# First batch of a spectral-filter and gated-FFN kernel: interleaved filter rows in larger pieces, the last two units loaded to both halves, one product on GpSimd

## Chip, cores and metric

One core of one Trainium2 chip. The time is device microseconds of one execution; "the loop" below is the long steady part that follows the first batch. The kernel before takes 782.3 us.

## The reference

```python
def _attn_ref(x, filt_r, filt_i):            # x (8, 3008, 256), filters (1505, 256), float32
    X = np.fft.rfft(x, axis=1)
    Y = X * (filt_r + 1j * filt_i)[None]
    return np.fft.irfft(Y, n=x.shape[1], axis=1).astype(np.float32)

def _moe_ref(x, w_in, w_out, beta):          # 24064 tokens, 256 -> 2048 -> 256
    h = x @ w_in
    g = h * (1.0 / (1.0 + np.exp(-beta * h)))
    return (g @ w_out).astype(np.float32)
```

The transforms are matmuls against sine tables made on the chip. Batch 0 goes through its transform first (the head, about 34 us). Then comes a loop of 752 steps, in which the FFN of one block runs beside the transform of the next batch.

## The kernel before

`fr_sb` and `fi_sb` hold the filters as [128 partitions, 24 rows, 256] float32. Partitions 0 to 63 and 64 to 127 carry the real and the imaginary part of the spectrum, so each filter value is needed in both halves. SyncE loads `fr` into the upper half and `fi` into the lower one; GpSimd copies each to the other half (`spread`). Six units of four rows go through VectorE. Further names: `t2` is one of the sine tables, `w_in` and `w_out` are the FFN's weights, `xg` is a piece of the second batch's input, Silu is the FFN's activation (one per loop step). An eviction is a copy of a matmul's result out of the accumulator memory, and the seam is the place where the head ends and the loop begins.

```python
    def load_filters(k0, k1):
        n = k1 - k0
        for filt, dst, p0 in ((filt_r, fr_sb, M), (filt_i, fi_sb, 0)):          # M = 64, H = 32
            for q0, off, sg in ((p0, k0, 1), (p0 + H, N1 - k0, -1)):
                src = AP(filt.tensor, filt.offset + off * D, [[N1 * D, H], [sg * D, n], [1, D]])
                nc.sync.dma_start(dst[q0 : q0 + H, k0:k1, :], src)
    ...
    for u in range(NUN):                                   # NUN = 6, KU = 4: 24 loads of 128 KB
        load_filters(u * KU, (u + 1) * KU)
    ...
    def s2_0(u):                                           # a unit: 4 matmuls, 2 products
        ...
        nc.vector.tensor_tensor(pq[u, 0][:], ps[:], fr_sb[:, ks, :], ALU.mult)
        nc.vector.scalar_tensor_tensor(pq[u, 1][:], ps[:], rot[:], fi_sb[:, ks, :], ALU.mult, ALU.mult)

    def spread(u):
        ks = slice(u * KU, (u + 1) * KU)
        nc.gpsimd.tensor_copy(fr_sb[:M, ks, :], fr_sb[M:, ks, :])
        nc.gpsimd.tensor_copy(fi_sb[M:, ks, :], fi_sb[:M, ks, :])

    for u in range(4):                                     # GpSimd's queue, in this order
        spread(u)
    load_win(0, 4 * P)                                     # w_in, cast to bf16 by the DMA
    spread(4)
    load_win(4 * P, FF)
    spread(5)
    for g in range(4):
        load_x(1, g)                                       # the second batch's input
    ...
    s2_0(3); unit(2); s2_0(4); a0_turn(5); ...; unit(3); s2_0(5); ...; unit(4)
```

Of the kernel before, what the change touches and what calls it, by code (L numbers as in the profile page):

```python
# [10 lines left out]
P = 128  # L11
# [10 lines left out]
N1 = 47  # L22
M = 64
# [13 lines left out]
def kernel(  # L37
# [45 lines left out]
    WZ = KP * J  # L83
    CH = M * J

    def load_filters(k0, k1):
        n = k1 - k0
        for filt, dst, p0 in ((filt_r, fr_sb, M), (filt_i, fi_sb, 0)):
            for q0, off, sg in ((p0, k0, 1), (p0 + H, N1 - k0, -1)):
                src = AP(filt.tensor, filt.offset + off * D, [[N1 * D, H], [sg * D, n], [1, D]])  # L90
                nc.sync.dma_start(dst[q0 : q0 + H, k0:k1, :], src)  # L91

    t1 = consts.tile([NP, KP], BF16, name="t1", tag="t1")
    t4 = consts.tile([KP, NP], BF16, name="t4", tag="t4")
# [46 lines left out]
    def iota(tile_, pattern, base=0, ch=0):  # L141
        nc.gpsimd.iota(tile_, pattern=pattern, base=base, channel_multiplier=ch)
# [39 lines left out]
    iota(kc[:], [[1, NK], [0, 2]])  # L182
    iota(cc[:], [[0, NK], [1, 2]], base=1)
    load_x0(8, 16)
    iota(vi[:, :, :H], [[1, NK], [N1, H]])
    load_x0(16, 24)
    iota(vi[:, :, H:], [[1, NK], [-N1, H]], base=N1 * (M - 1))
    load_x0(24, 28)
    make_identity(nc, ident)
    load_x0(28, 32)  # L190
# [2 lines left out]
    def shift_and(name, sh, mask, eng=None):  # L193
        t = small(name, I32)
        eng = eng or nc.vector
        if sh:
            eng.tensor_scalar(t[:], ip[:], sh, mask, ALU.logical_shift_right, ALU.bitwise_and)
        else:
            eng.tensor_scalar(t[:], ip[:], mask, None, ALU.bitwise_and)
        return t  # L200

    def affine(name, src, mul, add, eng=None):
        t = small(name)
        (eng or nc.vector).tensor_scalar(t[:], src[:], mul, add, ALU.mult, ALU.add)
        return t
# [10 lines left out]
    ms = affine("ms", shift_and("m_i", 0, M - 1), TURN / S, 0.0)  # L216
    off = affine("off", c_i, -TURN / 4, TURN / 4)
    q_i = shift_and("q_i", 0, 1)
    v_i = shift_and("v_i", 5, 1)
    q_p = (affine("q0", q_i, -1.0, 1.0), affine("q1", q_i, 1.0, 0.0))  # L220

    def t2_half(hi):
        t = sq.tile([P, NK, H], I32, name="u", tag=f"u{hi}")
        nc.vector.tensor_scalar(  # L224
            t[:], vi[:, :, hi * H : (hi + 1) * H], ms[:], off[:], ALU.mult, ALU.add
        )
        fold(t[:])
        nc.scalar.activation(
            t2[:, :, hi * H : (hi + 1) * H], t[:], ACT.Sin, scale=TWO_PI / TURN
        )  # L230

    def t2_shift(hi):
        for c in range(2):
            d0, s0 = (0, M) if c == 0 else (M, 0)
            dst = t2[d0 : d0 + M, :, M + hi * H : M + (hi + 1) * H]
            src = t2[s0 : s0 + M, :, hi * H : (hi + 1) * H]
            if c == hi:
                nc.vector.tensor_scalar_mul(dst, src, -1.0)
            else:
                nc.vector.tensor_copy(dst, src)  # L240

    MG = 4
    aTv = aT[:].rearrange("p e k (g m) -> p g e k m", m=MG)
# [64 lines left out]
    t2_half(1)  # L308
    seen = sp.tile([1, 2], BF16, name="seen", tag="seen")
    nc.sync.dma_start(seen[:], t2[:1, 1, M - 2 : M])  # L310
    for u in range(NUN):
        load_filters(u * KU, (u + 1) * KU)
    gp = nc.gpsimd
    rot = affine("rot", v_i, 2.0, -1.0, gp)
    tiny = sp.tile([P, NFB], F32, name="tiny", tag="tiny")
    gp.tensor_tensor(tiny[:], beta_sb[:], beta_sb[:], ALU.mult)
    gp.tensor_scalar(tiny[:], tiny[:], 1e-12, 2e-6, ALU.is_lt, ALU.mult)
# [1 line left out]
    s1_0(0, (False,))  # L319
    s1_0(1, (True,))  # L320
    spin(5, idle)
    t2_shift(0)
    t2_shift(1)
    nc.vector.memset(t2[:, 0, M : P : M - 1], 0.0)
    nc.scalar.activation(warm[:], ms[:], ACT.Silu)
    s1_0(2, (False,))
# [96 lines left out]
    r_p0 = ExitStack()  # L423
    p0pool = rpool("p0pool", r_p0, bufs=2, **tw)

    def s2_0(u):
        ps = bank2([P, KU, D])
        for i in range(KU):
            k1 = u * KU + i
            nc.tensor.matmul(ps[:, i, :], lhsT=t2[:, k1, :], rhs=a0[:, k1, :], start=True, stop=True)  # L430
        ks = slice(u * KU, (u + 1) * KU)
        for c in range(2):
            pq[u, c] = p0pool.tile([P, KU, D], BF16, name="pq_t", tag=f"pq{c}")
        nc.vector.tensor_tensor(pq[u, 0][:], ps[:], fr_sb[:, ks, :], ALU.mult)
        nc.vector.scalar_tensor_tensor(
            pq[u, 1][:], ps[:], rot[:], fi_sb[:, ks, :], ALU.mult, ALU.mult
        )
# [32 lines left out]
# [4 lines that stand above are left out]
# [6 lines left out]
    for u in range(4):  # L480
        spread(u)
    load_win(0, 4 * P)
    spread(4)
    load_win(4 * P, FF)
    spread(5)
    for g in range(4):
        load_x(1, g)
    load_wout(0)
    load_wout(WG)
    scale_wout(0)  # L490
    scale_wout(WG)

    s2_0(0)
    a0_turn(2)
# [3 lines left out]
    unit(0)  # L498
    a0_turn(3)
    s2_0(2)  # L500
    unit(1)
    a0_turn(4)
    s2_0(3)
    unit(2)
    s2_0(4)
    a0_turn(5)
    t3_part(2, True)
    t3_neg(2, True)
    unit(3)
    s2_0(5)  # L510
    idle = tpsum.tile([P, 512], F32, name="tps", tag="tps")
    spin(3, idle)
    unit(4)
    banks.close()

# [156 lines left out]
    for b in range(1, B):  # L672
        o = first_step[b - 1]
        if b == 1:
            at(0, z_late, 1, 0)
            at(1, z_late, 1, 1)
            s1_steps(1, range(16), [1 + (2 * i + 1) // 3 for i in range(16)], False, (1, 4, 7, 10, 13))
            for i, r in enumerate((11, 12, 13, 14)):
                at(r, f_late, 1, i // 2, i % 2)
            for g in range(NG):  # L680
                at(o + 13, a2_load, 1, g)
            for hh, z0, f0 in ((2, (13, 14), (15, 16, 17, 18)), (3, (18, 19), (20, 21, 22, 23))):
                for e in range(NDC):
                    at(z0[e], z_late, hh, e)
# [144 lines left out]
```

## Time and profile before

| kernel before | value | read from |
|---|---|---|
| time | 782.3 us (782.1 to 783.2) | runs |
| span of the profiled run | 780.2 us | page |
| filter loads land | 12.5 to 26.7 us | landing times in the trace |
| VectorE's last product of the head ends | 30.61 us | timeline |
| first transpose, first loop matmul | 31.44, 33.84 us | timeline of PE |
| granted clock | 1.00 throughout the head | stretches |

A timeline row gives the start, the duration, engine, line and operation, and in square brackets the idle time before it with what ended that. A "stretch" row gives the window, its length, busy time of PE, PE's weight loads, VectorE, ScalarE and GpSimd, then the granted TensorE clock, the DMA engines' busy share and GB/s. A DMA packet is called unslowed when it takes as long as between 42 and 45 us of this kernel: 159 ns (median) for 4096 bytes. The lines that carry the argument are in the prediction below.

### The profile page before, as it was taken

Reading aid. Unit: us, or ns where it says so; the run is one execution under the profiler, and the core shown is the slowest. Engines: PE = TensorE matmul, PEld = TensorE weight load, DVE = VectorE, ACT = ScalarE, POOL = GpSimd, SP = SyncE. Lnnn points to the kernel's source line nnn. Section 1 sums busy time; section 2 is a strip of 40 time slices with the busy share of each in tenths; the row PEclk is TensorE's granted clock in tenths of the full one; section 3 lists DMA queues with packets and bytes.
Section 4 is the critical chain, followed back from the end, with each engine's and each line's share of the span. In section 5 each row is a group of like instructions: output and inputs, shape, how many; then the busy total and the mean of one; then the engine's idle time right before and its main releaser. Section 6 shows DMA issues by size and latency. Waiting matters only on the chain.

```text
span 780.2 us, 15154 instructions
## 1 busy us (share of the span) xinstructions
PE 764.1 (98%) x5956; PEld 544.0 (70%) x6051; DVE 446.0 (57%) x713; ACT 552.6 (71%) x814; POOL 151.4 (19%) x155
## 2 busy tenths in 40 slices
PE   8899999999999999999999999999999999999997
PEld 5677667766776667866678666776667776676665
DVE  7869754766556665566546665567655666321001
ACT  6767877676677766777667776677766777777776
POOL 6714400312012210122201322022200222000000
PEclk9999999999999999999999999999999999999999
DMA  9975585244913358042671417622164111500101
GB/s 185 233 213 116 147 209 155 70 108 115 252 42 80 103 116 242 29 113 71 152 207 45 119 48 181 176 75 69 48 189 135 48 48 49 156 28 28 55 28 55
DMA packets 84411, 88.51 MB, mean 113 GB/s; under 512 B 5788, under 2 KB 74652, under 8 KB 84340
## 3 DMA queue, kind: packets, MB, share of 16 engines
q1 hardware_dynamic: 79892, 73.81, 32.0%
q0 software_dynamic: 4304, 13.60, 10.5%
q8 instruction: 47, 0.77, 0.4%
q14 instruction: 24, 0.20, 0.1%
q10 hardware_dynamic: 144, 0.13, 0.0%
HBM read 54.47 MB, written 46.66 MB: 130 GB/s over the span
## 4 chain that ended last, share of the span: by engine, by line
PE 94%; DMA 2%; issue 1%; POOL 1%; DVE 1%; SPq 0%; ACT 0%; DVEq 0%; POOLq 0%
PE acc L788 43%; PE hps L770 39%; PE ps L561 3%; PE ps L629 3%; PE ps L607 3%; PE ps L577 2%; DMA xg<-in_x_dram 1%; DMA fi_sb<-in_filt_i_dram 1%; POOL fi_sb L473 0%; POOL fr_sb L472 0%; SPq L91 0%; PE ps L405 0%; PE tp L400 0%; DVE y L114 0%; DVE u L224 0%
## 5 line engine op out<-in xcount | busy, mean ns | idle before, releaser
L779 ACT ACTIVATE gT<-hps,beta_sb 128x512 bf16<-128x512 f32 x752 | 516.9, 687 | 213.3 <-PE hps L770 191.9
L788 PE MATMUL acc<-wout_sb,gT 128*128 128x256 bf16 x3008 | 452.9, 272 | 2.3
L770 PE MATMUL hps<-y,win_sb 128*128 128x512 bf16 (+7 forms) x1636 | 428.0, 350 | 0.1
L788 PEld LDWEIGHTS <-gT 128*128 128x128 bf16 x3008 | 286.9, 98 | 121.6 <-issue 0.9
L596 POOL TENSOR_TENSOR yh<-a_t,b_t 128x512 bf16<-128x512 f32 x84 | 106.4, 1267 | 424.1 <-DVE b_t L595 422.8
L770 PEld LDWEIGHTS <-win_sb 128*128 128x128 bf16 x1728 | 164.8, 98 | 25.2 <-issue 0.9
L112 DVE COPY ost<-acc 128x512 f32<-128x512 f32 (+1 forms) x94 | 59.9, 679 | 138.3 <-PE acc L788 138.2
L112 DVE CAST a<-ps 96x512 bf16<-96x512 f32 x107 | 72.9, 685 | 53.3 <-PE ps L561 49.3
L114 DVE TENSOR_SCALAR y<-ps 128x376 bf16<-128x376 f32 (+2 forms) x128 | 63.3, 510 | 61.2 <-PE ps L629 57.9
L591 DVE TENSOR_TENSOR a_t<-ps,fr_sb 128x512 f32<-128x512 f32 x84 | 58.1, 692 | 67.0 <-PE ps L577 66.5
L592 DVE SCALAR_TENSOR_TENSOR b_t<-ps,fi_sb 64x512 f32<-64x512 f32 x84 | 58.2, 693 | 1.1
L595 DVE TENSOR_TENSOR b_t<-ps,fi_sb 64x512 f32<-64x512 f32 x84 | 57.4, 683 | 1.1
L112 DVE CAST z<-ps 128x512 bf16<-128x512 f32 x72 | 49.3, 684 | 1.7 <-PE ps L607 0.8
L629 PEld LDWEIGHTS <-zz 96*128 96x128 bf16 x448 | 29.7, 97 | 22.9
L561 PE MATMUL ps<-xg,t 94*96 94x512 bf16 x112 | 41.9, 381 | 1.5 <-DMA xg<-in_x_dram 0.8
L629 PE MATMUL ps<-t,zz 96*128 96x94 bf16 x448 | 34.7, 205 | 0.7
L607 PE MATMUL ps<-yh,t 128*128 128x256 bf16 x168 | 32.1, 273 | 0.6
L577 PE MATMUL ps<-a,t 128*128 128x256 bf16 x168 | 32.1, 273 | 0.3
L607 PEld LDWEIGHTS <-t 128*128 128x128 bf16 x168 | 16.2, 98 | 17.7 <-issue 0.7
L577 PEld LDWEIGHTS <-t 128*128 128x128 bf16 x168 | 16.1, 98 | 16.3
L171 POOL DMA_DIRECT2D xg<-in_x_dram x24 | 12.5, 521 | 56.7 <-PE ps L561 56.7
L561 PEld LDWEIGHTS <-t 94*96 94x96 bf16 x112 | 13.8, 123 | 10.3
(95 smaller groups left out, 177.3 us busy)
## 6 DMA issues: line engine op xcount, KB each, us to landing
out_dram<-ost SPq DMA_DIRECT2D x42, 512.0 KB, 3.0
d<-a SPq DMA_DIRECT2D x28, 384.0 KB, 5.1
a<-d SPq DMA_DIRECT2D x28, 384.0 KB, 4.9
d<-z SPq DMA_DIRECT2D x28, 384.0 KB, 3.9
zz<-d SPq DMA_DIRECT2D x28, 384.0 KB, 7.1
xg<-in_x_dram POOLq DMA_DIRECT2D x24, 384.0 KB, 6.3
out_dram<-ost SPq DMA_DIRECT2D x9, 256.0 KB, 3.8
ws<-in_moe_w_out_dram SPq DMA_DIRECT2D x4, 512.0 KB, 6.6
```

The source lines that it names most:

```text
L112: nc.vector.tensor_copy(dst, src)
L114: nc.vector.tensor_scalar_mul(dst, src, scale)
L561: nc.tensor.matmul(ps[:KP], lhsT=t1[:], rhs=xg[b, g][:NP, jj : jj + 2, :], start=True, stop=True)
L577: nc.tensor.matmul(ps[:, e, :], lhsT=t2[:, k0 + e, :], rhs=st["a2", b, g][:, kk + e, :], start=True, stop=True,)
L591: nc.vector.tensor_tensor(a_t[:], ps[:], fr_sb[:, ks, :], ALU.mult)
L592: nc.vector.scalar_tensor_tensor(b_t[:M], ps[M:], -1.0, fi_sb[M:, ks, :], ALU.mult, ALU.mult)
L596: nc.gpsimd.tensor_tensor(yh[:], a_t[:], b_t[:], ALU.add)
L607: nc.tensor.matmul(ps[:, e, :], lhsT=t3[:, 2 * i + e, :P], rhs=yh[:, e, :], start=True, stop=True)
L629: nc.tensor.matmul(ps[:, e, :NP], lhsT=zz[:, j0 % JG + e, dc * P : (dc + 1) * P], rhs=t4[:], start=True, stop=True,)
L770: nc.tensor.matmul(hps[:, pos - t0 : pos - t0 + ln], lhsT=win_sb[:, dc, fb * P : (fb + 1) * P], rhs=ys[b][:, dc, n0 : n0 + ln], start=(dc ...
L779: nc.scalar.activation(gT[:], hps[:], ACT.Silu, scale=beta_sb[:, fb : fb + 1])
L788: nc.tensor.matmul(acc_of(i, tb)[:, tb % 2, :], lhsT=blk[i * NFB + fb][:, tb * P : (tb + 1) * P], rhs=wout_sb[:, fb, :], start=(fb == 0 an ...
```

## The change

Its intent: fewer GpSimd copies and one VectorE product fewer, and loads that span 64 partitions (every second one) in place of 32 neighbours. Units 4 and 5 are loaded twice, so they need no copy; unit 4's second product goes to GpSimd, by way of a ScalarE eviction. The tables that depend on the row order are made to match.

```diff
-    def load_filters(k0, k1):
-        for filt, dst, p0 in ((filt_r, fr_sb, M), (filt_i, fi_sb, 0)):
-            for q0, off, sg in ((p0, k0, 1), (p0 + H, N1 - k0, -1)):
+    def load_filters(k0, k1, halves):
+        for hi, off, sg in ((0, k0, 1), (1, N1 - k0, -1)):
+            for (filt, dst), p0 in zip(FILTERS, halves):
                 ...
-                nc.sync.dma_start(dst[q0 : q0 + H, k0:k1, :], src)
+                nc.sync.dma_start(dst[p0 + hi : p0 + M : 2, k0:k1, :], src)
@@ (t2's index order; its sign shift as two int32 exclusive-ors in place of four bf16 operations) @@
-    for u in range(NUN):
-        load_filters(u * KU, (u + 1) * KU)
+    for k0, k1 in ((0, KU), (KU, KH), (KH, DUP), (DUP, NK)):      # 4, 4, 8, 8 rows
+        load_filters(k0, k1, (M, 0))
+    load_filters(DUP, NK, (0, M))                                 # DUP = 16: units 4, 5 again
@@ s2_0 @@
+        if on_pool:
+            nc.scalar.activation(zc[:], ps[:], ACT.Copy, scale=rot[:])
         nc.vector.tensor_tensor(pq[u, 0][:], ps[:], fr_sb[:, ks, :], ALU.mult)
+        if on_pool:
+            return
@@ GpSimd's queue @@
     load_win(0, 4 * P)
-    spread(4)
     load_win(4 * P, FF)
-    spread(5)
-    for g in range(4):
-        load_x(1, g)
+    load_x(1, 0)
@@ the units: a0_turn one unit earlier, unit(2) after s2_0(4), unit(3) after s2_0(5), scale_wout moved back @@
+    s2_0(4, True)
+    pool_product(4)                  # two gpsimd.tensor_tensor of 128x512
+    for g in range(1, 4):
+        load_x(1, g)
@@ the loop: second batch's first transform one step later, four late pieces in steps 2 to 5 @@
```

More of the change, by code (lines that the diff above doesn't have):

```diff
@@ L84 @@
     CH = M * J
-    def load_filters(k0, k1):
-        n = k1 - k0
-        for filt, dst, p0 in ((filt_r, fr_sb, M), (filt_i, fi_sb, 0)):
-            for q0, off, sg in ((p0, k0, 1), (p0 + H, N1 - k0, -1)):
-                src = AP(filt.tensor, filt.offset + off * D, [[N1 * D, H], [sg * D, n], [1, D]])
-                nc.sync.dma_start(dst[q0 : q0 + H, k0:k1, :], src)
+    FILTERS = ((filt_r, fr_sb), (filt_i, fi_sb))
+    DUP = 2 * KH
+    def load_filters(k0, k1, halves):
+        for hi, off, sg in ((0, k0, 1), (1, N1 - k0, -1)):
+            for (filt, dst), p0 in zip(FILTERS, halves):
+                src = AP(filt.tensor, filt.offset + off * D, [[N1 * D, H], [sg * D, k1 - k0], [1, D]])
+                nc.sync.dma_start(dst[p0 + hi : p0 + M : 2, k0:k1, :], src)
     t1 = consts.tile([NP, KP], BF16, name="t1", tag="t1")
@@ L184 @@
     load_x0(8, 16)
-    iota(vi[:, :, :H], [[1, NK], [N1, H]])
+    viv = vi[:].rearrange("p k (m h) -> p k m h", h=2)
+    iota(viv[:, :, :, 0], [[1, NK], [N1, H]])
     load_x0(16, 24)
-    iota(vi[:, :, H:], [[1, NK], [-N1, H]], base=N1 * (M - 1))
+    iota(viv[:, :, :, 1], [[1, NK], [-N1, H]], base=N1 * (M - 1))
     load_x0(24, 28)
@@ L218 @@
     q_i = shift_and("q_i", 0, 1)
-    v_i = shift_and("v_i", 5, 1)
     q_p = (affine("q0", q_i, -1.0, 1.0), affine("q1", q_i, 1.0, 0.0))
@@ L224, in t2_half @@
         nc.vector.tensor_scalar(
-            t[:], vi[:, :, hi * H : (hi + 1) * H], ms[:], off[:], ALU.mult, ALU.add
+            t[:], viv[:, :, :, hi], ms[:], off[:], ALU.mult, ALU.add
         )
@@ L228, in t2_half, with t2_shift @@
         nc.scalar.activation(
-            t2[:, :, hi * H : (hi + 1) * H], t[:], ACT.Sin, scale=TWO_PI / TURN
-        )
-    def t2_shift(hi):
-        for c in range(2):
+            t2[:, :, :M].rearrange("p k (m h) -> p k m h", h=2)[:, :, :, hi],
+            t[:],
+            ACT.Sin,
+            scale=TWO_PI / TURN
+        )
+    def t2_shift():
+        pairs = t2[:].rearrange("p k m -> p (k m)").bitcast(I32).rearrange("p (k m) -> p k m", k=NK)
+        for c, bit in enumerate((1 << 15, -(1 << 31))):
             d0, s0 = (0, M) if c == 0 else (M, 0)
-            dst = t2[d0 : d0 + M, :, M + hi * H : M + (hi + 1) * H]
-            src = t2[s0 : s0 + M, :, hi * H : (hi + 1) * H]
-            if c == hi:
-                nc.vector.tensor_scalar_mul(dst, src, -1.0)
-            else:
-                nc.vector.tensor_copy(dst, src)
+            nc.vector.tensor_scalar(
+                pairs[d0 : d0 + M, :, H:], pairs[s0 : s0 + M, :, :H], bit, None, ALU.bitwise_xor
+            )
     MG = 4
@@ L310 @@
     nc.sync.dma_start(seen[:], t2[:1, 1, M - 2 : M])
-    for u in range(NUN):
-        load_filters(u * KU, (u + 1) * KU)
+    for k0, k1 in ((0, KU), (KU, KH), (KH, DUP), (DUP, NK)):
+        load_filters(k0, k1, (M, 0))
+    load_filters(DUP, NK, (0, M))
     gp = nc.gpsimd
-    rot = affine("rot", v_i, 2.0, -1.0, gp)
+    rot = affine("rot", q_i, 2.0, -1.0, gp)
     tiny = sp.tile([P, NFB], F32, name="tiny", tag="tiny")
@@ L321 @@
     spin(5, idle)
-    t2_shift(0)
-    t2_shift(1)
+    t2_shift()
     nc.vector.memset(t2[:, 0, M : P : M - 1], 0.0)
@@ L424, with s2_0 @@
     p0pool = rpool("p0pool", r_p0, bufs=2, **tw)
-    def s2_0(u):
+    zc = sr.tile([P, KU, D], F32, name="zc", tag="zc")
+    def s2_0(u, on_pool=False):
         ps = bank2([P, KU, D])
@@ L482, with pool_product @@
     load_win(0, 4 * P)
-    spread(4)
     load_win(4 * P, FF)
-    spread(5)
-    for g in range(4):
-        load_x(1, g)
+    load_x(1, 0)
+    def pool_product(u):
+        for i in range(0, KU, 2):
+            k0 = u * KU + i
+            nc.gpsimd.tensor_tensor(
+                pq[u, 1][:, i : i + 2, :], zc[:, i : i + 2, :], fi_sb[:, k0 : k0 + 2, :], ALU.mult
+            )
     load_wout(0)
     load_wout(WG)
-    scale_wout(0)
-    scale_wout(WG)
     s2_0(0)
@@ L500 @@
     s2_0(2)
+    a0_turn(4)
     unit(1)
-    a0_turn(4)
     s2_0(3)
+    a0_turn(5)
+    s2_0(4, True)
+    pool_product(4)
+    for g in range(1, 4):
+        load_x(1, g)
+    scale_wout(0)
+    scale_wout(WG)
     unit(2)
-    s2_0(4)
-    a0_turn(5)
     t3_part(2, True)
     t3_neg(2, True)
-    unit(3)
     s2_0(5)
@@ L512 @@
     spin(3, idle)
+    unit(3)
     unit(4)
@@ L676 @@
             at(1, z_late, 1, 1)
-            s1_steps(1, range(16), [1 + (2 * i + 1) // 3 for i in range(16)], False, (1, 4, 7, 10, 13))
-            for i, r in enumerate((11, 12, 13, 14)):
+            s1_steps(1, range(16), [2 + (2 * i + 1) // 3 for i in range(16)], False, (1, 4, 7, 10, 13))
+            for i, r in enumerate((2, 3, 4, 5)):
                 at(r, f_late, 1, i // 2, i % 2)
             for g in range(NG):
-                at(o + 13, a2_load, 1, g)
+                at(o + 14, a2_load, 1, g)
             for hh, z0, f0 in ((2, (13, 14), (15, 16, 17, 18)), (3, (18, 19), (20, 21, 22, 23))):
```

## The prediction

What the text below said of the hardware without a trace or run of this case is cut, and the cuts are marked. No term of its sum is among them: it comes to 782.3 - 1.1 = 781.2 us with a load rate of 0.31 MB/us, an estimate between the 231 and 323 GB/s of the stretches. GpSimd's 1.27 us for a product of 128x512 is the mean of its `yh` product in the trace of the kernel before (1267 ns).

> **What bounds the kernel now.** I read the page first: where is TensorE (PE) not full? These are its slices (each 19.5 us) of PE and of the DMA engines, and the summary of the chain that ended last.
>
> ```profile
> PE   8899999999999999999999999999999999999997
> ...
> DMA  9975585244913358042671417622164111500101
> ...
> PE 94%; DMA 2%; issue 1%; POOL 1%; DVE 1%; SPq 0%; ACT 0%; DVEq 0%; POOLq 0%
> ```
>
> PE is full from the third slice to the end, and the chain lies on PE for 94%. The change leaves the matmuls of the long loop alone, so what it can win lies in the first two slices: the first batch, which must be finished before the loop starts. That puts a ceiling on it: the first loop matmul starts at 33.84 us of a 780.2 us span, and even 2% (15.6 us) is half of that head. Then the timeline of PE near the seam:
>
> ```profile
> 30.68 0.62 PE L444 MATMUL lp<-t,pq_t 128*128 128x128 bf16 x8 [0.57 <-DVE pq_t L435]
> 31.44 1.07 PE L400 MATMUL zp<-ident,y 128*128 128x128 bf16 x16
> ...
> 33.84 0.59 PE L770 MATMUL hps<-y,win_sb 128*128 128x512 bf16 x2
> ...
> 36.61 0.38 PE L561 MATMUL ps<-xg,t 94*96 94x512 bf16 x1 [0.84 <-DMA xg<-in_x_dram]
> ```
>
> The last unit's matmuls wait for VectorE's last product; transposes follow at 31.44 us, the loop at 33.84. In the loop's ramp PE waits once, 0.84 us, for the second batch's first input piece. After that step times (from one Silu to the next) agree with the work in them, so PE never waits again worth a mention. So the time is the loop's start plus a constant, plus that stall. What sets the loop's start? VectorE's timeline:
>
> ```profile
> 24.19 1.27 DVE L435 SCALAR_TENSOR_TENSOR pq_t<-sps,rot,fi_sb 128x1024 bf16<-128x1024 f32 x1
> 25.38 1.21 DVE L434 TENSOR_TENSOR pq_t<-sps,fr_sb 128x1024 bf16<-128x1024 f32 x1
> 26.52 1.27 DVE L435 SCALAR_TENSOR_TENSOR pq_t<-sps,rot,fi_sb 128x1024 bf16<-128x1024 f32 x1
> 28.20 1.22 DVE L434 TENSOR_TENSOR pq_t<-sps,fr_sb 128x1024 bf16<-128x1024 f32 x1 [0.41 <-POOL fr_sb L472]
> 29.34 1.27 DVE L435 SCALAR_TENSOR_TENSOR pq_t<-sps,rot,fi_sb 128x1024 bf16<-128x1024 f32 x1
> ```
>
> Six units, two products each, follow one another from 16.08 us to 30.61, about 1.16 us start to start; only once does VectorE wait 0.41 us, for GpSimd (POOL) which copies the filters to the other 64 partitions. The chain of waits shows that GpSimd's queue is paced just as tightly, and the filter loads before it:
>
> ```profile
> 12.68 5.16 DMA fi_sb<-in_filt_i_dram
> ...
> 20.22 0.97 POOL fi_sb L473
> 21.19 0.12 issue
> 21.32 0.99 POOL fr_sb L472
> ...
> 28.62 0.59 issue
> 29.21 7.35 DMA xg<-in_x_dram
> 36.56 0.04 issue
> ```
>
> So three chains run level: loads (2 x 256 KB per unit), copies (2 x 1.04 us), products (2 x 1.16 us). Shortening one alone gives little. Last, how fast the loads are: a table by stretch of the filter loads, the w_out loads, the second batch's loads, and stores in the loop.
>
> ```profile
> 13.00:25.00 12.00, 10.59 (x145) 8.71 (x143) 10.97 (x13) 10.28 (x13) 9.80 (x10) 1.00 1.02 231
> 25.50:28.00 2.50, 1.67 (x16) 1.15 (x16) 2.29 (x2) 2.47 (x4) 2.45 (x3) 1.00 1.11 323
> 29.00:36.50 7.50, 5.90 (x76) 4.32 (x75) 6.01 (x14) 4.85 (x9) 6.02 (x7) 1.00 1.09 211
> 42.00:45.00 3.00, 2.96 (x19) 1.88 (x19) 1.43 (x3) 2.17 (x4) 1.02 (x1) 1.00 1.07 375
> ```
>
> The last two columns are DMA share and GB/s. The engines are full in all, but the filters run at 231 GB/s where w_out (128 partitions) gets 323. The trace's packet durations say the same: in the filter stretch a 4096-byte packet takes 285 ns in the mean, against 159 ns (median) at 42 to 45 us. (The third row counts the bf16 bytes of loads that read f32.)
>
> [...] But stores from 64 partitions at 57.7 us have a median of 159 ns for 4096 bytes, unslowed[...]. [...] (yh, 128x512: 1267 ns, against 692 for VectorE's a_t).
>
> **The change part by part.**
> - *One product to GpSimd.* Removes one VectorE product (1.16 us net) and, with the copies for units 4 and 5 gone, the 0.41 us wait. It adds one ScalarE eviction of 128x1024 (1.02 us, as its other ones; ScalarE has gaps of 0.4 to 1.1 us between 20 and 29 us that take most of it) and two GpSimd products of 128x512, 2 x 1.27 = 2.5 us.
> - *Copies.* Four of 1.04 us leave GpSimd. Both win loads and the first input piece are then issued by about 25 us, where the last win load and that piece went out at 26.37 and 29.21.
> - *Loads.* Units 4 and 5 are loaded twice: 3.15 MB become 4.19 MB. In time at 231 GB/s that is 1.05/0.231 = 4.5 us more. Pieces grow from 128 to 256 KB beyond unit 1 (20 issues for 24; SyncE spends about 0.43 us on one and waits 2.0 us in all for landings).
> - *t2's sign shift.* Four bf16 VectorE instructions (about 0.36 us each, 1.43) become two int32 ones; from the folds of the same element count (0.61 to 0.71) I estimate 1.3. PE waits for ScalarE there, so nothing on the path.
> - *Loop schedule.* The same work at other steps; a late head piece costs VectorE 2 x 0.31 us in steps 2 to 5, beside about 0.69 of eviction, under PE's 1.26 to 1.47 us per step. No new wait there.
>
> The sum, with T the moment when unit 4's first product can start. VectorE is free at 25.46 us; the doubled fr must have landed too. From T: 1.2 us to that product's end; about 0.65 us because the reordered unit 3 needs the bank that this product frees, and unit 5's product needs the buffer that unit 3 frees; two products (2.45 to 2.5 us); then PE, eviction and the first transpose about 1.05 us, when ScalarE finishes unit 4's eviction, itself held by GpSimd's product, at about the same time. So transposes start near T + 5.4 us, against 31.44. Break-even is T = 26.05.
> T hangs on the load rate. The first filter DMA lands at 12.46 us; the rest follows at a rate R. For fr of the double to land, about 3.8 MB more must have: at R = 0.32 MB/us T is free of the loads (24.3, so 25.46), start -0.6 us; at 0.28 T = 26.0, start 0; at 0.234 T = 28.7, start +2.7 us. The input stall: in the kernel before the first input piece lands 9.9 us after the last filter (36.56 against 26.7), with the same w_out and win loads between; I keep that distance, and it is needed 2.2 us after the loop's start (two steps of 0.88 and one matmul pair). At 0.32 the filters end at 12.46 + 4.06/0.32 = 25.1, the piece lands at 35.0, needed at 35.4: the 0.84 is saved, total -0.6 - 0.84 = -1.4 us. At 0.28 it lands at 36.9, needed at 36.0: total about 0. At 0.234: 39.7 against 38.7, total about +2.9.
>
> I choose a rate near 0.31, between the 231 of now and w_out's 323: spreading over 64 partitions has the stores' evidence behind it, and doubling the loads makes sense only to someone who saw them speed up. That gives about -1.1 us: 782.3 - 1.1 = 781.2.
>
> **Rivals.**
> (a) *The loads stay at 231 GB/s*: [...] the double arrives near 29.7 us and becomes the wait that takes the place of the GpSimd copies. For it: [...] full DMA engines; against: the 64-partition stores. Time about 785.
> (b) *GpSimd's product becomes the bound*: it starts only when fi's double lands, takes 2.5 us, and ScalarE's eviction (1.02) follows. For it: that estimate leaves no slack; against: it starts near T. About 781.5 to 782.5.
> (c) *The input piece stays the wait*: DMA is full up to 45 us, the megabyte added pushes it, and the loop's earlier start is given back as a longer stall. For it: DMA share of 1.09 from 29 to 36.5 us. About 782.3.
> (d) *All goes through*: loads over 330 GB/s, T = 25.46, stall gone, and a little more from VectorE: about 780.3.
>
> **Range and chances.** (d) and (a) are the ends that I take seriously; 8 in 10 lies between 779.9 and 784.0. No branch comes near 15.6 us, so the chances are 0.01 faster, 0.985 within 2%, 0.005 slower.
>
> **What would show it.** In the changed kernel: GB/s between 13 and 25 us (about 300 if I am right, 231 for rival a); what unit 4's first product waits for, and its start (25.5 to 26); the last VectorE product's end (29.5 to 30.2 against 30.61); the first L400 transpose (about 30.9 to 31.3), the first hps matmul (about 33.3), and the wait ahead of the first matmul on xg (under 0.4 us). The prediction is wrong if the loads do not speed up, if t2 or the first unit comes later than 16.1 us (strided reads on VectorE are unmeasured here), or if PE waits again in steps 2 to 12.

## The result

The changed kernel takes 786.4 us (median; 785.8 to 787.3) beside 782.3 us for the kernel before. The ratio is 1.0051 with a 95% interval of 1.0033 to 1.0068. (Ratios are the mean time of one kernel's fast runs over that of the other's fast runs of the same rounds, so not quite the ratio of the medians.) It is correct. So: within 2% as said, but 4 us slower, outside the range of 779.9 to 784.0, and in the other direction than 781.2.

First the page of the changed kernel: PE's and the DMA engines' slices, and the summary of the chain that ended last.

```profile
PE   8699999999999999999999999999999999999997
DMA  8975686233831349123480426713164211500101
PE 94%; DMA 2%; SPq 1%; issue 1%; DVE 1%; POOL 0%; ACT 0%; DVEq 0%; POOLq 0%
```

The loop's slices are full as before. The second slice fell from 8 to 6: all that happened lies in the head. Next its stretches: the early filter loads, the rest of them, and what comes after.

```profile
13.00:17.00 4.00, 3.59 (x43) 2.61 (x42) 2.95 (x6) 3.18 (x6) 1.96 (x2) 1.00 0.77 209
17.00:31.00 14.00, 9.20 (x125) 7.79 (x124) 9.49 (x9) 11.51 (x13) 8.39 (x10) 1.00 1.05 234
31.30:38.10 6.80, 5.26 (x46) 4.54 (x47) 3.66 (x6) 1.98 (x4) 5.93 (x6) 0.50 1.12 241
```

Two things answer the prediction at once. The rate in the long stretch is 234 GB/s, about as in the kernel before (231), with the engines full (1.05). (In the first row they are not, 0.77: there the pieces are still of 128 KB, and SyncE starts one per 0.65 us, which is 0.20 MB/us.) And in the third row PE's granted clock is 0.50. VectorE's timeline shows what the rate does:

```profile
22.20 1.23 DVE L441 TENSOR_TENSOR pq_t<-sps,fr_sb 128x1024 bf16<-128x1024 f32 x1 [1.22 <-POOL fr_sb L481]
...
30.33 2.36 DVE L441 TENSOR_TENSOR pq_t<-sps,fr_sb 128x1024 bf16<-128x1024 f32 x2 [3.25 <-DMA fr_sb<-in_filt_r_dram]
```

Unit 4's first product waits 3.25 us for the second load of `fr` and starts at 30.33, not at 25.5 to 26 (the row joins it with unit 5's first product, which follows at once). There is a smaller new wait of 1.22 us at unit 2. The chain that ended last runs through that load:

```profile
17.02 5.26 DMA fi_sb<-in_filt_i_dram
...
22.30 9.16 DMA fi_sb<-in_filt_i_dram
...
31.71 2.50 POOL pq_t L498 x2
...
34.26 0.82 PE sps L453 x6
35.08 1.71 PE lp L453 x16
36.79 1.66 PE zp L403 x16
```

Read it upward from the bottom: the transposes follow the last units' matmuls, those wait for GpSimd's product, and that starts when the last filter load lands, 9.16 us after its issue at 22.30. (The load at 17.02 ahead of it is the wait of the issuing queue for an earlier landing.) Last, PE at the seam:

```profile
34.88 1.91 PE L453 MATMUL lp<-t,pq_t 128*128 128x128 bf16 x16
36.73 1.70 PE L403 MATMUL zp<-ident,y 128*128 128x128 bf16 x16
...
40.00 0.59 PE L787 MATMUL hps<-y,win_sb 128*128 128x512 bf16 x2 [0.32 <-ACT y L112]
...
42.19 0.38 PE L578 MATMUL ps<-xg,t 94*96 94x512 bf16 x1
```

Transposes come 5.29 us later than before, and the loop's first matmul 6.16 us later (40.00 against 33.84), because the way between the two takes 3.27 us in place of 2.40. Of these 0.87 us some 0.6 go with the half clock: a_filled2 and a_spin below, with the same order of work at full clock there, take 2.67. The half clock also costs time before the transposes: unit 4's last 16 matmuls (first row) take 1.91 us, in a_spin 1.06. The first matmul on `xg` no longer waits, which returns the 0.84 us, but not because its data come sooner: that piece lands at 41.55 us, 5.0 later than before, and the loop is later still. From step 16 to the end every Silu comes 5.16 to 5.18 us later than before. The profiled span is only 4.4 us longer: after the last Silu that run's tail was 0.8 us shorter, which I did not look into.

### The profile page after: what moved, and what is told of

Same layout as the page of the kernel before. It is cut to its first block, busy times and chain, and to the rows that moved or that the text cites. A ratio compares the mean times of both kernels' runs of the same rounds, so it can differ in the third digit from the quotient of the medians.

```text
span 784.6 us, 15139 instructions
## 1 busy us (share of the span) xinstructions
PE 765.6 (98%) x5955; PEld 545.6 (70%) x6051; DVE 444.9 (57%) x709; ACT 553.8 (71%) x815; POOL 149.8 (19%) x153
## 3 DMA queue, kind: packets, MB, share of 16 engines
q1 hardware_dynamic: 80276, 74.86, 32.3%
## 4 chain that ended last, share of the span: by engine, by line
PE 94%; DMA 2%; SPq 1%; issue 1%; DVE 1%; POOL 0%; ACT 0%; DVEq 0%; POOLq 0%
PE acc L805 43%; PE hps L787 39%; PE ps L578 3%; PE ps L646 3%; PE ps L624 3%; PE ps L594 2%; DMA fi_sb<-in_filt_i_dram 2%; SPq L93 1%; PE tp L403 0%; POOL pq_t L498 0%; PE ps L408 0%; PE lp L453 0%; DVE u L226 0%; PE zp L403 0%; DVE u L147 0%
## 5 line engine op out<-in xcount | busy, mean ns | idle before, releaser
L646 PEld LDWEIGHTS <-zz 96*128 96x128 bf16 x448 | 29.7, 97 | 22.9
L646 PE MATMUL ps<-t,zz 96*128 96x94 bf16 x448 | 34.7, 205 | 0.8
L624 PEld LDWEIGHTS <-t 128*128 128x128 bf16 x168 | 16.2, 98 | 17.7 <-issue 0.7
L594 PEld LDWEIGHTS <-t 128*128 128x128 bf16 x168 | 16.1, 98 | 16.3
```

Of the source, the lines that this page charges most:

```text
L594: nc.tensor.matmul(ps[:, e, :], lhsT=t2[:, k0 + e, :], rhs=st["a2", b, g][:, kk + e, :], start=True, stop=True,)
L624: nc.tensor.matmul(ps[:, e, :], lhsT=t3[:, 2 * i + e, :P], rhs=yh[:, e, :], start=True, stop=True)
L646: nc.tensor.matmul(ps[:, e, :NP], lhsT=zz[:, j0 % JG + e, dc * P : (dc + 1) * P], rhs=t4[:], start=True, stop=True,)
```

## The experiments

All runs compared here are timed in rounds beside the kernel before on the same chip. "Shift" is how much later the loop runs than in the kernel before, from the profiled run alone. As the half clock falls differently from one profile to another (31.28 to 38.10 us in the changed kernel, 25.1 to 28.5 in a_spin) and the runs of one kernel differ, the medians decide.

| run | what | median us (before) | ratio, 95% |
|---|---|---|---|
| a_copied | changed, no second load, all six units copied | 787.59 (782.15) | 1.0069, 1.0057 to 1.0081 |
| a_vector | changed, unit 4's product back on VectorE | 787.37 (782.15) | 1.0064, 1.0051 to 1.0077 |
| b_rows | before, interleaved rows only | 787.44 (782.15) | 1.0069, 1.0055 to 1.0083 |
| b_order | before, fr and fi issued in turn | 782.13 (782.15) | 0.9999, 0.9987 to 1.0011 |
| a_contig | changed, contiguous rows | 785.63 (782.23) | 1.0040, 1.0027 to 1.0052 |
| a_filled | changed, second load replaced by fills (wrong result) | 783.11 (782.23) | 1.0014, 1.0002 to 1.0026 |
| a_spin | changed, PE kept busy | 786.95 (782.23) | 1.0075, 1.0057 to 1.0093 |
| b_pieces | before, larger pieces only | 783.79 (782.23) | 1.0023, 1.0011 to 1.0034 |
| a_filled2 | as a_filled, fills elsewhere (wrong result) | 783.47 (782.25) | 1.0018, 1.0006 to 1.0031 |
| b_wide | before, loads over 128 partitions (wrong result) | 782.55 (782.25) | 1.0004, 0.9991 to 1.0018 |
| b_queue | b_order, GpSimd's queue reordered | 782.83 (782.25) | 1.0008, 0.9996 to 1.0021 |
| b_queue2 | b_queue with the changed loop steps | 781.80 (782.25) | 0.9999, 0.9986 to 1.0011 |
| b_double | b_order with the second load alone | 790.89 (782.04) | 1.0108, 1.0090 to 1.0125 |
| a_both | changed, contiguous rows and 128 KB pieces | 790.90 (782.04) | 1.0107, 1.0092 to 1.0122 |
| a_small | changed, 128 KB pieces | 794.06 (782.04) | 1.0150, 1.0132 to 1.0167 |
| b_held | b_double, GpSimd's loads after the filters | 787.05 (782.19) | 1.0063, 1.0040 to 1.0085 |

The first theory was: the megabyte loaded twice, at an unchanged rate, is the whole loss. Its rivals: the interleaved rows or the larger pieces slow the loads by themselves, GpSimd's product is the bound, or the half clock is.

**a_copied: no second load.**

```diff
-    load_filters(DUP, NK, (0, M))
@@
-    for u in range(4):
+    for u in range(NUN):
         spread(u)
```

> The changed kernel without the double load: GpSimd copies units 4 and 5 as in the kernel before; its product stays on GpSimd. Theory bytes (the doubled 1.05 MB at a rate that stayed near 230 GB/s made unit 4 wait): unit 4's first product starts near 27 us instead of 30.3, GpSimd's product comes after its copies (about 30 to 32.4), time 783 to 784. Theory rows (the interleaved rows make the loads slow or late by themselves): 785.5 or more. Theory product (GpSimd's product is the cost): 785 or more, as it now comes behind four more copies.

787.59 us, no gain. The last filter landed at 26.86 us, as in the kernel before, so the loads were as short as wanted. But GpSimd's queue now held four more copies: its w_in loads were issued at 30.2 and 31.0 us in place of 25.6, and its product began near 32.3. The test moved the wait to another engine and so decides nothing on the bytes.

**a_vector: unit 4's second product on VectorE.**

```diff
-    s2_0(4, True)
-    pool_product(4)
+    s2_0(4)
```

> The changed kernel with unit 4's second product back on VectorE, the double load kept. Theory bytes: VectorE still waits till 30.3 us, ends near 35.1; first transpose within 0.6 us of 36.7; time 785.8 to 787. Theory product (GpSimd's 2.5 us behind the last load are the cost): 784.5 or less.

787.37 us. The time does not fall, so moving the product back is no cure. That does not make it free: VectorE then does a fourth product after the late load. (The profiled run was the slowest of the five, 789.71 us.)

**b_rows: interleaved rows in the kernel before.**

```diff
-            for q0, off, sg in ((p0, k0, 1), (p0 + H, N1 - k0, -1)):
+            for hi, off, sg in ((0, k0, 1), (1, N1 - k0, -1)):
-                nc.sync.dma_start(dst[q0 : q0 + H, k0:k1, :], src)
+                nc.sync.dma_start(dst[p0 + hi : p0 + M : 2, k0:k1, :], src)
@@ (t2's tables and sign shift as in the change) @@
```

> The kernel before with interleaved rows (and what goes with them in t2) and nothing else. Theory bytes: 782 to 783, filters at 225 to 240 GB/s. Theory rows: issue of a filter DMA takes 0.6 us instead of 0.43 and the time is 784 or more.

787.44 us: the rows alone cost 5.3 us, so the theory of the bytes as the only cost fell here. The queue that issues the loads shows why. First two issues of a unit in the kernel before where it waits for nothing, then in b_rows:

```profile
13.14 0.89 SPq L91 DMA_DIRECT2D fr_sb<-in_filt_r_dram  x2
```

```profile
18.39 1.26 SPq L93 DMA_DIRECT2D fr_sb<-in_filt_r_dram  x2
```

An issue takes 0.60 to 0.62 us in place of 0.43. 24 of them at about 0.65 us start to start are 15.6 us, and the last filter lands at 31.48 us in place of 26.70. From 17 us on packets of 4096 bytes had a median of 159 ns, that of an unslowed one, and the DMA engines were 0.54 to 0.69 busy between 13 and 25 us: they were not the limit any more, the issuing engine was. The last four loads suffered from something else as well: they took 4.5 to 5.9 us from issue to landing, where the ones before took 2.6 to 3.8. GpSimd had issued w_in at 24.23, and its packets had 58% of the engines' time from 26 to 28 us; b_double below shows what that does. How the 5.3 us divide between the two was not tested. VectorE then waits for the copies, three times like this:

```profile
30.39 1.22 DVE L436 TENSOR_TENSOR pq_t<-sps,fr_sb 128x1024 bf16<-128x1024 f32 x1 [1.67 <-POOL fr_sb L474]
```

**b_order: the same pieces, issued in turn.**

```diff
-        for filt, dst, p0 in ((filt_r, fr_sb, M), (filt_i, fi_sb, 0)):
-            for q0, off, sg in ((p0, k0, 1), (p0 + H, N1 - k0, -1)):
+        for hi, off, sg in ((0, k0, 1), (1, N1 - k0, -1)):
+            for filt, dst, p0 in ((filt_r, fr_sb, M), (filt_i, fi_sb, 0)):
+                q0 = p0 + hi * H
```

> The kernel before with fr and fi pieces issued in turn, nothing else. If alternating between the two partition halves lets the loads overlap, the rate between 13 and 22 us rises to 280 GB/s or more and the last filter lands before 25 us instead of 26.7; if they serialize, it stays at 225 to 240. Either way VectorE's products bound: 781.7 to 783.

782.13 us, the same time. The rate rose to 247 and 255 GB/s between 13 and 21 us and the last filter landed at 25.60, 1.1 us earlier. Loads that come earlier win nothing there, as the copies (2 x 1.04 us a unit) and products (2 x 1.16) are paced level with them.

**a_contig: the changed kernel with contiguous rows.**

```diff
-                nc.sync.dma_start(dst[p0 + hi : p0 + M : 2, k0:k1, :], src)
+                nc.sync.dma_start(dst[p0 + hi * H : p0 + (hi + 1) * H, k0:k1, :], src)
@@ (t2's tables and sign shift as before the change) @@
```

> The changed kernel with contiguous rows again (t2 part as before), all else of the change kept: alternating halves, larger pieces, double, GpSimd product. If the rows are most of the loss: issues of about 0.42 us, packets mostly at their unslowed 46 and 159 ns, 250 GB/s or more between 17 and 29 us, the doubled fr lands near 27.7 instead of 30.1, time 782.5 to 784. If the doubled bytes alone are it: the rate stays at 225 to 235, fr lands at 29 or later, time 784.5 to 786.5.

785.63 us: about 0.8 us come back (the intervals of the two ratios overlap, so the size is not firm). Most issues take 0.42 us again, but the rate stays at 236 to 246 GB/s with slowed packets (1024 bytes: 75 ns in place of 46), and the wait for the second load stands:

```profile
29.09 2.36 DVE L441 TENSOR_TENSOR pq_t<-sps,fr_sb 128x1024 bf16<-128x1024 f32 x2 [3.15 <-DMA fr_sb<-in_filt_r_dram]
```

So in the changed kernel the larger pieces (20 issues for 4.19 MB) hide most of what the rows cost in b_rows.

**a_filled and a_filled2: no second load, the other halves filled with a constant.** These take the bytes away without adding copies. a_filled fills on GpSimd in the setup; a_filled2 moves the fills to gaps of GpSimd.

```diff
-    load_filters(DUP, NK, (0, M))
+    nc.gpsimd.memset(fr_sb[:M, DUP:NK, :], 0.05)
+    nc.gpsimd.memset(fi_sb[M:, DUP:NK, :], 0.05)
```

> Wrong results on purpose: the changed kernel without the double load; the other halves of units 4 and 5 are filled with a constant by GpSimd in the setup (about 2 us where it is idle), so nothing waits for the 1.05 MB and nothing else changes. Theory bytes: unit 4's first product starts at about 26.7 us (its own half and VectorE's place), GpSimd's product begins near 27 us, the loop starts 33 to 34, time 781 to 782.5. Theory rows alone: the pieces still land late and the time stays above 784.

783.11 us, but GpSimd's two fills (1.80 and 2.10 us) stood in the way of VectorE's sign shift of t2, which took 4.08 us in place of the changed kernel's 1.12 (fills from 8.49 to 12.44 us, the shift from 8.78 to 12.86):

```profile
8.78 4.08 DVE L241 TENSOR_SCALAR t<-t 64x768 int32<-64x768 int32 x2 [0.27 <-ACT t L230]
```

> Wrong results on purpose, as a_filled, but with the fills placed where they do not hold up VectorE (the first fill blocked its sign shift for 3 us and started unit 0 1.6 us late). Theory bytes: unit 0 at 16.25 us as in the changed kernel, unit 4's first product by 26.7, time 781.0 to 782.3. If the time stays above 783.5, something other than the double's bytes costs.

783.47 us, and the first unit at 16.2 us as in the changed kernel. VectorE's timeline:

```profile
23.09 1.23 DVE L441 TENSOR_TENSOR pq_t<-sps,fr_sb 128x1024 bf16<-128x1024 f32 x1 [1.96 <-POOL fr_sb L481]
...
27.79 1.21 DVE L441 TENSOR_TENSOR pq_t<-sps,fr_sb 128x1024 bf16<-128x1024 f32 x1
29.68 1.23 DVE L441 TENSOR_TENSOR pq_t<-sps,fr_sb 128x1024 bf16<-128x1024 f32 x1 [0.67 <-PE sps L453]
```

Without the second load unit 4 waits for nothing, the clock stays at 1.0, and 2.9 us come back (2.6 by the ratios). What is left against the kernel before is 1.2 us. It shows in the first row: unit 2 waits 1.96 us for a piece of 256 KB. (In the changed kernel it waits 1.22. In this run the piece landed at 21.91 us in place of 21.01; one load ahead of it had taken 1.75 us to issue, where the longest took 0.90 in the changed kernel's profile.) The third row is the buffer wait of unit 5 on unit 3 that the prediction put at 0.65 us.

**a_spin: PE kept busy, to see whether the clock stays.**

```diff
+    spin(10, idle)
-    unit(4)
+    unit(4, 4)              # four idle matmuls between the unit's two halves
```

> The changed kernel with 14 more idle matmuls where PE waits for the double (10 ahead of unit 4, 4 between its halves), so that PE does not stand still there. If PE's pause is what halves the granted clock from 31.3 to 38.1 us, the clock stays at 1.0 and the loop starts 0.8 to 1.3 us earlier: 785.0 to 785.7. If the clock falls anyway or costs nothing: 786.0 to 787.

786.95 us: no gain. In the profiled run the half clock lay elsewhere (25.1 to 28.5 us), so PE's last part was faster:

```profile
35.46 1.06 PE L455 MATMUL lp<-t,pq_t 128*128 128x128 bf16 x16
```

From the end of GpSimd's product to the loop's first matmul it took 4.52 us (35.05 to 39.57), in the changed kernel's profile 5.80 (34.20 to 40.00). So the half clock after PE's wait costs about 1.3 us there. Two things hid the gain in this run: the last filter load landed at 32.31 us in place of 31.46, and PE waited 0.48 us for `xg`. Two of six runs took over 790 us. What the half clock costs in the median stays open; I could not cash it.

**b_pieces: larger pieces in the kernel before.**

```diff
-    for u in range(NUN):
-        load_filters(u * KU, (u + 1) * KU)
+    for k0, k1 in ((0, KU), (KU, KH), (KH, 2 * KH), (2 * KH, NK)):
+        load_filters(k0, k1)
```

> The kernel before with the larger pieces (4, 4, 8, 8) and nothing else: contiguous rows, fr before fi. If piece size is harmless: 782 to 783. If the wait for a whole 256 KB pair holds up units 2 and 3 (VectorE waited 1.22 us there in the changed kernel): unit 2 waits 0.3 to 1 us, 782.7 to 783.5. Rate between 17 and 25 us 230 to 240 GB/s if packets set it, 260 or more if the eight outstanding loads do.

(The eight outstanding loads: in the changed kernel the twentieth filter load is issued at 22.30 us, when the twelfth, issued at 17.02, has landed at 22.28.)

783.79 us: 1.6 us slower, at 206 to 235 GB/s with packets slowed more (1024 bytes: 86 ns). A unit cannot start before its whole piece has come: unit 2's two products wait 0.99 and 1.13 us for copies of such pieces.

**b_wide: is it the partitions?** Every filter load spans 128 partitions (half the rows, used twice; wrong result), same bytes and number of loads.

```diff
-                nc.sync.dma_start(dst[q0 : q0 + H, k0:k1, :], src)
+                src = AP(filt.tensor, filt.offset + (k0 + i) * D, [[11 * D, P], [1, D]])
+                nc.sync.dma_start(dst[:, k0 + i, :], src)
```

> Wrong results on purpose: the kernel before with every filter DMA spread over 128 partitions (128 KB each as before, same number of them, same copies and products in size). If the 32-partition destinations hold the rate near 230 GB/s, it rises to 290 GB/s or more between 13 and 21 us and the last filter lands before 24 us instead of 26.7. If the eight outstanding loads or HBM hold it: 230 to 250. Time 781.3 to 782.4 either way, as VectorE bounds.

782.55 us. Nearly all packets were unslowed (46 ns for 1024 bytes) and the DMA share fell to 0.83 to 0.87, but the rate was only 245 to 258 GB/s: one load of 0.131 MB per 0.47 us, start of issue to start of issue, is at most 0.28 MB/us. So with loads of this size, issued at this pace from one queue, 0.31 was out of reach, whatever the partitions.

**b_queue and b_queue2: use what was learned.** No second load; unit 5's copies and the first `xg` go ahead of the second w_in load. b_queue2 adds the changed kernel's loop steps.

```diff
-    load_win(4 * P, FF)
     spread(5)
-    for g in range(4):
+    load_x(1, 0)
+    load_win(4 * P, FF)
+    for g in range(1, 4):
         load_x(1, g)
```

> A candidate: the kernel before with fr and fi in turn, and on GpSimd's queue unit 5's copies ahead of the second win load and the second batch's first piece ahead of it too. VectorE's wait of 0.41 us goes and the input stall of 0.84 shrinks: 780.8 to 781.7 if both are on the path, 782 or more if the second win load becomes the wait in step 4.

> The same candidate with the changed kernel's loop steps (head pieces at steps 2 to 5, second batch one step later). If the input piece still makes PE wait in b_queue, this fills that time: 0.2 to 0.8 us faster than b_queue; otherwise the same within 0.3.

782.83 and 781.80 us, both the same as before. VectorE's 0.41 us wait and the 0.84 us stall on the first `xg` piece went. The second w_in load came later (38.1 and 37.3 us, before 34.7) but cost PE at most 0.25 us. The wait moved to the second `xg` piece, now behind w_in: it landed at 40.33 and 40.58 us (before 38.74), and PE waited 1.61 us for it in b_queue, 0.78 in b_queue2:

```profile
40.38 0.63 PE L563 MATMUL ps<-xg,t 94*96 94x512 bf16 x2 [1.61 <-DMA xg<-in_x_dram]
```

DMA is 1.02 to 1.05 busy from 29 to 45 us in b_queue: moving a load forward moves another back.

**b_double: the second load alone.** Here I wanted the three shares (bytes, pieces, rows) one by one.

```diff
     for u in range(NUN):
         load_filters(u * KU, (u + 1) * KU)
+    for u in (4, 5):
+        load_filters(u * KU, (u + 1) * KU, (0, M))
@@
-    spread(4)
     load_win(4 * P, FF)
-    spread(5)
```

> The kernel before with the filter pieces issued in turn (as in b_order, which changed no time) and with one part of the change alone: units 4 and 5 are loaded a second time into the other half, in pieces of 128 KB and contiguous rows, and the four GpSimd copies for them are gone. Theory (the doubled bytes are the largest share): at 0.25 MB/us the last filter lands 1.05/0.25 = 4.2 us later than b_order's 25.6, near 29.8; unit 4's double near 27.7 holds its product until then instead of 25.4, unit 5's second product starts near 31, and the loop starts 1.5 to 2.5 us later; less the 0.84 us stall, which goes, the time is 782.9 to 784.5. If the interleaved rows and larger pieces were the whole cost, the second loads would be free and the time 781.3 to 782.3.

790.89 us: far above what I expected. VectorE's last two units:

```profile
29.25 1.22 DVE L437 TENSOR_TENSOR pq_t<-sps,fr_sb 128x1024 bf16<-128x1024 f32 x1 [3.79 <-DMA fr_sb<-in_filt_r_dram]
31.59 1.28 DVE L438 SCALAR_TENSOR_TENSOR pq_t<-sps,rot,fi_sb 128x1024 bf16<-128x1024 f32 x1 [1.12 <-DMA fi_sb<-in_filt_i_dram]
36.66 1.23 DVE L437 TENSOR_TENSOR pq_t<-sps,fr_sb 128x1024 bf16<-128x1024 f32 x1 [3.78 <-DMA fr_sb<-in_filt_r_dram]
```

The filters issued up to 22.6 us had landed by 26.4. GpSimd, free of four copies, issued w_in at 22.74, and every filter load issued after that took until 29 to 38.8 us. The DMA queues between 26 and 29 us (packets, MB, share of the engines' time; software_dynamic is GpSimd's queue, hardware_dynamic SyncE's):

```profile
q0 software_dynamic: 230, 0.27, 75.9%
q1 hardware_dynamic: 149, 0.16, 19.5%
```

In the mean a packet of w_in's queue took 158 ns there and one of the filters' 63 (share times 3 us times 16 engines, over packets).

The same for the changed kernel between 26 and 31 us, where w_in had been issued at 25.58:

```profile
q1 hardware_dynamic: 842, 1.10, 104.4%
```

There the filters have the engines to themselves: all had been issued by 22.9 us, ahead of w_in, whose first packets run only after 31 us.

**a_both and a_small: undo pieces and rows in the changed kernel.**

```diff
-    for k0, k1 in ((0, KU), (KU, KH), (KH, DUP), (DUP, NK)):
-        load_filters(k0, k1, (M, 0))
-    load_filters(DUP, NK, (0, M))
+    for u in range(NUN):
+        load_filters(u * KU, (u + 1) * KU, (M, 0))
+    for u in (4, 5):
+        load_filters(u * KU, (u + 1) * KU, (0, M))
@@ (a_both: contiguous rows as in a_contig as well) @@
```

> The changed kernel with contiguous rows and 128 KB pieces for all, doubles too (unit 4's before unit 5's); doubled bytes, loop steps and the GpSimd product stay. Theory: the three costs (bytes, rows, pieces) are apart, so about 0.8 us (rows, from a_contig) and 1.2 to 1.6 us (pieces, from b_pieces and a_filled2) come back: 783.8 to 784.6, the last filter lands near 30, unit 2 does not wait, and unit 4's product starts near 27.7 instead of 30.3. If the bytes alone carried the loss it would stay at 785.5 or above, as a_contig.

> The changed kernel with 128 KB pieces, but still on interleaved rows: 32 loads at 0.65 us of issue each are 20.8 us from 9.6, so the last lands near 32 or later whatever the bytes. Theory (interleaved rows are issue-bound, and the larger pieces of the change are there to hide that): slower than the changed kernel, 787 to 789. If the issue time did not matter, smaller pieces would help as in a_both: 784 to 785.5.

790.90 and 794.06 us. The shares do not add: larger pieces cost 1.6 us in the kernel before, and in the presence of the second load they save 5.3 us (a_both against a_contig) and 7.6 us (a_small against the changed kernel). In both runs w_in went out (23.2 and 24.0 us) before the last filter loads were issued, and those landed up to 36.4 us in a_both; in a_small SyncE was still issuing after 30 us and the loads landed after 40.

**b_held: is it the company of w_in?**

```diff
+    held = sr.tile([P, 1], F32, name="held", tag="held")
+    nc.gpsimd.tensor_copy(held[M + H :], fi_sb[M + H :, NK - 1, :1])     # the last piece
     load_win(0, 4 * P)
```

> b_double (790.89 us, not the 783 to 784.5 that I expected) with one more GpSimd instruction: a copy of 32 elements from the piece that is issued last, ahead of the w_in loads, so that GpSimd issues w_in and x only after all filters have landed. In b_double the doubled pieces took 27.8 to 38.8 us to land, with w_in's packets among theirs from 26 us on. Theory (the doubled pieces lose their place to w_in and x): filters land by 29.5 to 30.5 us, VectorE's fifth unit starts at 27 to 28.5, the first transpose near 33 instead of 41 or later; w_in and x then come late and PE waits for them in the first steps, 1.5 to 3 us: 784.5 to 786.5. Rival (32 loads of 128 KB are slow by themselves): filters still land after 35 us and the time stays above 789.

787.05 us (785.4 to 791.0). First VectorE's last two units in this kernel, then PE in its first loop steps:

```profile
26.07 1.23 DVE L437 TENSOR_TENSOR pq_t<-sps,fr_sb 128x1024 bf16<-128x1024 f32 x1 [0.62 <-DMA fr_sb<-in_filt_r_dram]
...
30.22 1.23 DVE L437 TENSOR_TENSOR pq_t<-sps,fr_sb 128x1024 bf16<-128x1024 f32 x1 [1.74 <-DMA fr_sb<-in_filt_r_dram]
```

```profile
42.97 0.38 PE L564 MATMUL ps<-xg,t 94*96 94x512 bf16 x1 [3.28 <-DMA xg<-in_x_dram]
```

The same 32 loads land by 29.99 us, at 263 to 269 GB/s from 21 us on, and the first transpose is at 33.67 us in place of 41.20. So the company was the cause in b_double, and the rival (many loads are slow by themselves) falls. It also shows that 0.23 MB/us is no ceiling for loads into these halves. But w_in and `xg` come later by what was saved: PE waits 3.28 us for `xg`, and the shift grows from 3.9 us at the loop's start to 8.0 by its eighth step in that run. The gain against b_double is 3.8 us in the median; the time is still 4.9 us above the kernel before.

## Why the prediction was wrong

- **The step that failed** is "I choose a rate near 0.31, between the 231 of now and w_out's 323: spreading over 64 partitions has the stores' evidence behind it". From the first landing at 13.44 us to that of `fr`'s second load at 30.11, 3.80 MB came (4.19 less the first load of 0.13 and the last of 0.26): 0.228 MB/us, as low as my lowest branch. The first landing was also 1.0 us later than the 12.46 the sum starts from. The sum's own formula then holds roughly. With T = 30.33 it gives transposes at 35.7; they came at 36.73, and the half clock in PE's last matmuls (1.91 us for 1.06) accounts for most of the rest. (A slip beside it: at 0.31 the sum gives about -1.4 us, not -1.1. Nothing hangs on it.)
- **The evidence for 0.31 was of another kind.** Stores with unslowed packets say nothing of what the loads' issuing allows. Nor were they a test of 64 partitions: two stores, one from each half, were issued at 57.67 and 58.27 us and ran together. b_rows has unslowed packets too and is slower, for each issue takes 0.60 to 0.62 us. b_wide has 128 partitions and unslowed packets and reaches 258 GB/s at most; its pieces are of 128 KB, so it says nothing of larger ones. In the changed kernel, with larger pieces, the packets are slowed (1024 bytes 76 ns, 8192 bytes 548 ns, medians from 21 to 25 us, against 46 and an estimated 318, twice the 159 of a 4096-byte one) and the engines are full at 234 GB/s.
- **"Doubling the loads makes sense only to someone who saw them speed up"** was an argument about an author, not about the chip, and it tipped the choice.
- **Rival (a) is what happened**, with its number: I gave about 785 and 29.7 us for the second load of `fr`; it landed at 30.11. Its number came true; that the two halves bound the rate is not shown: with contiguous rows the same bytes went into the same halves at 236 to 246 GB/s (a_contig) and, in pieces of 128 KB, at 263 to 269 (b_held). a_filled2 shows the second load to cost 2.9 us of the 4.1 (2.6 by the ratios). The other 1.2 us is there without it: units wait for whole pieces (1.22 us at unit 2, and b_pieces alone costs 1.6), and the rows cost about 0.8 us (a_contig, not firm). These sizes come from different kernels and do not add up, as a_both and a_small show.
- **Rival (b) came as a part of (a):** GpSimd's product starts only with `fi`'s second load (31.46 us) and ends at 34.2, and PE's last matmuls of unit 4 wait 0.83 us for it. Without it (a_vector) the time is no better. Its 2.49 us are the 2.5 worked out.
- **Not foreseen:** the half clock after PE's wait, about 1.3 us in the changed kernel's profile (see a_spin). It lasts from 31.28 to 38.10 us (granted 0.50); in the 3.41 us before it PE was busy for 1.37, and PE's idle time of 2.32 us ended at 31.61. What sets it off was not shown. Also not foreseen: the longer issues, and what order does. The large pieces, which I counted only as fewer issues, are what keeps the second load ahead of w_in.
- **Right by luck:** the 0.84 us stall is saved. I had the `xg` piece land at 35.0 us, sooner than before; it lands at 41.55 and is in time only because the loop begins at 40.00.
- **Right:** that only the head changes; PE waits nowhere new in steps 2 to 12; unit 5's buffer wait (0.67 us in a_filled2 for an estimated 0.65); t2's sign shift 1.12 us, where 1.3 was estimated. The first unit came at 16.25 us in place of 16.08, just past the 16.1 that I had named; b_rows (16.24) shares that and a_contig (16.07) does not, so it goes with the interleaved rows; it is small beside the rest.
- **Open:** why the packets of 256 KB pieces are slowed (a_contig, 75 ns for 1024 bytes at 236 to 246 GB/s), where those of 128 KB pieces, also in turn to the two halves, mostly were not (b_order, 247 and 255 GB/s); why one of the sixth to eleventh filter loads takes 0.9 to 1.75 us to issue in every kernel (1.24 us at 14.08 in the kernel before, beside 0.43 for most others); and how the 1.2 us divides between pieces and rows. The changed kernel with contiguous rows, small pieces and w_in held back, which would join what b_held and a_both showed, was not run.

No version beat the kernel before: b_queue2 with 781.80 against 782.25 us lies within its interval. In the kernel before the DMA engines are full from 13 to 45 us (a share of 1.02 to 1.13 in the stretches that cover it), so a megabyte more costs about 1.05/0.234 = 4.5 us somewhere (an estimate from the stretches). Issuing fr and fi in turn (b_order) lowers their share to 0.83 and 0.86 between 13 and 21 us, but the w_out, w_in and `xg` loads that follow fill them again, and there order only chooses which engine waits.

## What to carry to other kernels

Before loading data twice to save copies, ask whether the DMA engines are full until the point where the loop's own inputs land. Here they were (a share of 1.02 to 1.13), and the bytes added came back as a wait (3.25 us at unit 4). The freed engine may also issue its own loads earlier, into the same engines: b_double's GpSimd issued w_in from 22.74 us on, where the kernel before did at 23.40 and 26.37, and its queue had 75.9% of the engines' time from 26 to 29 us. The rate of a new access shape had three limits here, to be checked one by one: packet duration (76 ns for 1024 bytes in the changed kernel, 46 unslowed), issue time per load (0.60 to 0.62 us in b_rows, 0.43 before), and which other queue is in company (b_double, 790.89 us; b_held, 787.05). Reading the packet duration alone would not have been enough: in b_rows the packets were unslowed, and the time was 5.3 us longer. To judge a part of a change, undo it in the changed kernel as well as adding it to the old one: the larger pieces cost 1.6 us in one and saved over 5 us in the other, where they kept the loads ahead of another queue's.
